# Hedgehog linear attention with a gated GLU on one core: the GLU's products in three passes over both chunks of tokens, with partial sums in DRAM

## The chip, the core and the metric

The kernel runs on one core of one Trainium2 chip. The core has five engines with a queue of instructions each: PE (TensorE, matmuls into the banks of PSUM), DVE (VectorE), ACT (ScalarE), POOL (GpSimd) and SP (SyncE, which issues the DMA transfers here). Each engine takes its own instructions strictly in order and waits on semaphores for those of the others. The metric is the device time of one execution in microseconds (us), as the median of several runs.

## What is computed

x has 2048 rows (tokens) of 1024 numbers. The layer norm of x feeds two branches that are multiplied at the end.

```python
xn  = layernorm(x)
# branch A: linear attention, 32 heads of 32
q, k, v = split(xn @ wqkv)
pq, pk  = per head: q @ w_phi, k @ w_phi
phi     = [softmax(p), softmax(-p)]          # 64 features for each head
kv, z   = phi_k.T @ v, sum(phi_k)            # over all 2048 tokens
s       = ((phi_q @ kv) / (phi_q @ z + 1e-6)) @ wo
# branch B: gated GLU, 1024 -> 3584 -> 1024
g   = silu((sigmoid(xn @ w_gate) * (xn @ w_up)) @ w_down)
out = x + s * g
```

All of it is in single precision. The sums over all tokens (kv, z) stand between the features of k and the rest of branch A.

## The kernel before

**Products.** Every factor of a large product is kept as two parts, a rounded high part and the rest (`split`, L128 to L131: an ACT cast makes the high part, L130, and a DVE subtraction the low one, L131). `mm3` (L133 to L137) multiplies with three matmuls: high by high, high by low, low by high. Each large product is cut in two along all three dimensions and done with seven block products in place of eight, named B11, T2, T3, B21, T1, T4, B22 (Strassen-Winograd). For that there are sums of blocks of the weights (made by POOL, `w_sums`, and stored in DRAM where they are used again), sums of blocks of the normalised x, and sums of results (DVE, while it empties the banks).

**Stages.** The 2048 tokens are two chunks of 1024. The order of the work is: projection of chunk 0 (V, K, Q), GLU of chunk 0, projection of chunk 1, GLU of chunk 1, the down product, then the attention's output and the store. The projection of chunk 0 with all that leads to it (loading, norm, transposes, folding w_phi into the weights of q and k) follows an order written out by hand, a list of short names, `FIRST` (L791 on); everything else is issued by loops and keeps the order of the program on each engine.

**The GLU of a chunk.** It runs over 14 column blocks j and two halves s. For each of these 28 pairs come the seven block products, each 12 matmuls of 512 columns into one bank from a ring of four. The factor from x lies in SBUF, split, for the whole chunk (28 slots of 512 KB, tiles x0 to x6). The weights go through eight slots (`w`, split, NW = 8): `prep` (L360) fills the next slot as soon as one is free. In chunk 0 it splits raw or summed weights and stores the four split sums to DRAM (`ws_d`); in chunk 1 it loads those four and splits the other three. Two partial sums u1 and u2 are kept in SBUF and added to by DVE from product to product (L1066 on); the gates, multiplications and sums of h blocks for the down product are ACT, DVE and POOL, and h goes to DRAM (`h_d`).

**Work in the background.** Beside the products run two lists of tasks, issued by `background` (L1008) behind a given DVE instruction. `bg` holds the features of q for chunk 0 and the transposing of x for chunk 1 (`q_features`, `x_task`, in the GLU of chunk 0), and then 32 `k_task`s (L462) with the sums behind them: for a tile of 128 tokens and half the heads it loads k and v, makes the two softmaxes (`features`, L440 to L457: maximum and minimum, two subtractions, exponential on ACT, a sum, a reciprocal), multiplies, splits p and v and adds to z. Its eight matmuls of 256 columns (`kv_products`, L481) are issued when the next task is issued. In the GLU of chunk 1 that is once in six products:

```python
            if m >= 1 and (m - 1) % 6 == 0:
                background(v.ins)
```

`bg2` holds sums of weights for wo and w_down (`o_sums`, `wd_sums`: four loads, four POOL operations, stores), one for each 14 products.

## Time and profile before

| | |
|---|---|
| time, median of 3 runs | 2377.14 us (2375.92 to 2377.75) |
| span of the profiled execution | 2376.2 us |
| mean granted TensorE clock | 1.00 |
| projection of chunk 0, from its first product's loads | about 14 to 286 us |
| GLU of chunk 0 | about 286 to 818 us |
| projection of chunk 1 | about 818 to 1053 us |
| GLU of chunk 1 | about 1053 to 1609 us |
| down product | about 1609 to 2128 us |
| attention and output | about 2128 us to the end |
| moved by DMA | 600 MB |

Engine rows of the page give busy time, share of the span and count of instructions. Rows of groups read: line, engine, operation, output<-input names, tile, count, busy us, mean ns of one, and what ended the idle time before them. Rows of waits read: waiting engine and line <- engine and line that released it, then the sum in us, the count and the longest. Rows of windows give the stretch, its length, the busy time (and count) of PE, weight load, DVE, ACT and POOL, the granted clock, the busy share of the DMA engines and GB/s. A bare timeline row gives start and duration in us. DMA rows give the count, the size of one and the median us from issue to landing.

### The profile page before, as it was taken

To read this page: it belongs to the slowest core of one execution; us is meant where nothing else is said; L and a number is where in the kernel's file an instruction comes from. 1 tells how busy PE (TensorE), PEld (TensorE's weight loads), DVE (VectorE), ACT (ScalarE), POOL (GpSimd) and SP (SyncE) were. 2 spreads that over 40 slices of the span, in tenths; PEclk is the share of its full clock that TensorE was granted. 3 is DMA by queue.
4 is the path that set the end of the run, shared out by engine and by line. 5 is a ranking of instruction groups with operands and counts; after the bars stand their busy time and mean duration, and the time that the engine had idled before them with its cause. 6 is when DMAs were issued, how large, how long until landed. Compare 5 with 4: busy or idle time off the path is not lost.

```text
span 2376.2 us, 31871 instructions
## 1 busy us (share of the span) xinstructions
PE 2361.1 (99%) x10972; PEld 1966.2 (83%) x10972; DVE 1778.2 (75%) x2340; ACT 1022.0 (43%) x1516; POOL 959.8 (40%) x613
## 2 busy tenths in 40 slices
PE   9999999999999999999999999999999999999999
PEld 8888888888888888888878888888888888888887
DVE  8626777877777575668884888865889998878776
ACT  7333344444434342324443444444444334455553
POOL 0223456666666433123443222232333334424566
PEclk9999999999999999999999999999999999999999
DMA  6689987778776787677777666668666666876665
GB/s 237 234 310 321 339 318 263 289 265 291 259 283 246 248 309 261 234 262 242 275 266 250 231 219 216 222 207 312 209 220 230 239 218 209 288 252 244 204 209 177
DMA packets 233587, 600.49 MB, mean 253 GB/s; under 512 B 30672, under 2 KB 30928, under 8 KB 228816
## 3 DMA queue, kind: packets, MB, share of 16 engines
q1 hardware_dynamic: 233424, 598.45, 72.3%
q8 instruction: 86, 1.41, 0.2%
q14 instruction: 77, 0.63, 0.1%
HBM read 363.20 MB, written 235.14 MB: 252 GB/s over the span
## 4 chain that ended last, share of the span: by engine, by line
PE 92%; DVE 4%; DMA 2%; issue 1%; ACT 1%; POOL 0%; SPq 0%; DVEq 0%; ACTq 0%
PE bank L135 29%; PE bank L137 29%; PE bank L136 29%; PE bank L696 1%; PE bank L672 1%; PE bank L486 1%; PE bank L285 1%; DMA fc<-wqkT 1%; DVE p L131 1%; DVE w L131 0%; DVE fc L450 0%; DVE fc L449 0%; DMA x<-x 0%; DMA fa<-wf_d 0%; DVE stk L453 0%
## 5 line engine op out<-in xcount | busy, mean ns | idle before, releaser
L136 PE MATMUL bank<-x,w 128*128 128x512 f32 x2352 | 915.7, 389 | 0.0
L135 PE MATMUL bank<-x,w 128*128 128x512 f32 x2352 | 909.8, 390 | 1.6 <-DVE fc L1073 1.1
L137 PE MATMUL bank<-x,w 128*128 128x512 f32 x2352 | 906.3, 390 | 0.0
L130 ACT CAST w<-fa 128x512 fp32r<-128x512 f32 (+1 forms) x430 | 294.8, 688 | 574.0 <-PE bank L136 365.9
L135 PEld LDWEIGHTS bank<-x,w 128*128 128x128 f32 x2352 | 441.6, 188 | 94.1 <-DVE fc L1073 2.3
L137 PEld LDWEIGHTS bank<-x,w 128*128 128x128 f32 x2352 | 441.5, 188 | 91.5 <-DVE w L131 0.4
L136 PEld LDWEIGHTS bank<-x,w 128*128 128x128 f32 x2352 | 441.6, 188 | 90.3
L131 DVE TENSOR_TENSOR w<-fa,w 128x512 fp32r<-128x512 f32 (+1 forms) x430 | 415.8, 972 | 104.1 <-ACT w L130 90.8
L135 PE MATMUL bank<-w,x 128*128 128x512 f32 x708 | 277.8, 393 | 0.2 <-ACT w L877 0.2
L136 PE MATMUL bank<-w,x 128*128 128x512 f32 x708 | 276.2, 390 | 0.9 <-DVE w L878 0.9
L137 PE MATMUL bank<-w,x 128*128 128x512 f32 x708 | 275.8, 390 | 0.0
L1089 POOL TENSOR_TENSOR fb<-fb,fc 128x512 f32<-128x512 f32 x57 | 89.0, 1561 | 291.6 <-DVE fc L1088 264.8
L137 PEld LDWEIGHTS bank<-w,x 128*128 128x128 f32 x708 | 132.9, 188 | 27.8 <-DVE x L868 0.3
L136 PEld LDWEIGHTS bank<-w,x 128*128 128x128 f32 x708 | 133.1, 188 | 27.4 <-DVE w L878 1.3
L135 PEld LDWEIGHTS bank<-w,x 128*128 128x128 f32 x708 | 133.1, 188 | 27.2 <-ACT w L877 0.6
L628 POOL TENSOR_TENSOR fc<-fc 128x1024 f32<-128x1024 f32 x32 | 81.4, 2542 | 173.7 <-ACT fc L451 125.4
L1088 DVE TENSOR_TENSOR fc<-fc,bank 128x512 f32<-128x512 f32 x84 | 57.5, 684 | 102.5 <-PE bank L137 97.4
L131 DVE TENSOR_TENSOR x<-fa,x 128x512 fp32r<-128x512 f32 x112 | 113.5, 1013 | 23.8 <-ACT x L130 23.6
L130 ACT CAST w<-fb 128x512 fp32r<-128x512 f32 x112 | 69.7, 622 | 141.7 <-PE bank L136 115.3
L131 DVE TENSOR_TENSOR p<-fc,p 128x1024 fp32r<-128x1024 f32 (+2 forms) x97 | 103.9, 1081 | 10.6 <-ACT p L130 8.3
L130 ACT CAST p<-fc 128x1024 fp32r<-128x1024 f32 (+2 forms) x97 | 70.7, 738 | 90.3 <-DVE fc L467 50.7
L640 POOL TENSOR_TENSOR fc<-fc,sa 128x1024 f32<-128x1024 f32 x32 | 70.4, 2199 | 90.6 <-DVE sa L637 90.6
(258 smaller groups left out, 3231.2 us busy)
## 6 DMA issues: line engine op xcount, KB each, us to landing
ws_d<-w SPq DMA_DIRECT2D x112, 512.0 KB, 4.2
w<-ws_d SPq DMA_DIRECT2D x112, 512.0 KB, 4.8
fa<-w_gu SPq DMA_DIRECT2D x84, 512.0 KB, 4.4
fa<-h_d SPq DMA_DIRECT2D x84, 512.0 KB, 4.0
fa<-wf_d SPq DMA_DIRECT2D x32, 1024.0 KB, 6.9
h_d<-fc SPq DMA_DIRECT2D x120, 256.0 KB, 3.2
fc<-e_d SPq DMA_DIRECT2D x48, 512.0 KB, 4.8
fc<-qkv_d SPq DMA_DIRECT2D x80, 256.0 KB, 4.3
```

The costliest lines, as they stand in the source:

```text
L130: nc.scalar.copy(o[0], src)
L131: return nc.vector.tensor_sub(o[1], src, o[0].bitcast(F32))
L135: nc.tensor.matmul(o, a[0], b[0], start=first, stop=False, **kw)
L136: nc.tensor.matmul(o, a[0], b[1], start=False, stop=False, **kw)
L137: nc.tensor.matmul(o, a[1], b[0], start=False, stop=last, **kw)
L285: nc.tensor.matmul(ps[:, gs], r[:, gs], bd[:, 4 * f + g], start=True, stop=True)
L486: nc.tensor.matmul(kvb[g // 2][:, g % 2 * 256:g % 2 * 256 + 256], v[:, g].rearrange("p a f -> p (a f)"), ph[:, g].rearrange("p a f -> p (a ...
L628: nc.gpsimd.tensor_mul(ez, e, zb)
L640: nc.gpsimd.tensor_mul(e3, e3, r2[:, :, None].to_broadcast([P, 32, DH]))
L672: nc.tensor.transpose(ps[:, j * P:(j + 1) * P], e[:, k * P:(k + 1) * P], ident)
L1088: v = nc.vector.tensor_add(b, u2 if q == 3 else u1, bank)
L1089: nc.gpsimd.tensor_mul(g, g, b)
```

## The change

The GLU is now made for both chunks of tokens together, product by product, in three passes over the 14 column blocks f:

- Pass 0 (after the projection of chunk 0): B11, B21 for each f, 28 units.
- Pass 1 (after the projection of chunk 1): T2, T3, T4, 42 units.
- Pass 2: T1, B22, 28 units.

A unit is one block product for both halves s and both chunks th of tokens: 48 matmuls into four fixed banks, with two weight slots, each used for both chunks. So each split weight serves both chunks: 196 splits where 280 stood, and no split weights in DRAM. `ws_d` gives way to `wg_d` for raw sums of weights, made by 28 new tasks in `bg2` (`glu_sums`: four loads, four POOL operations, four stores), which run from the projection of chunk 0 on to pass 1.

The factors from x are needed for both chunks at once, in three sets. Their raw blocks and sums go to DRAM in new stores (`xr_d`): 16 new entries X in the list `FIRST` and `outer_sums` in the `x_task`s. They come back through `load_outer` and `load_operand`: a load into a temporary slot (43 and 44, or 53 and 54) and a split.

The partial sums go to DRAM between the passes (`m_d`): after B11, T2 and T3 four ACT copies empty the banks and four stores keep them (`keep_banks`), `fetch` loads them a unit ahead, and T2 begins with four ACT copies of B11's sums into the banks. T3 and T4 go on in the same banks, B22 in T1's. `h_direct` (sigmoid on ACT, multiplication on DVE, straight from the banks) and `h_added` (four DVE additions of the kept sums, sigmoid, multiplication on POOL) make h.

The background moves too: `x_task`s go to pass 0, five k_tasks stay in the projection of chunk 1, the other 27 with the six tasks of sums go to the first 33 units of pass 1, one after each unit, and the 16 `q_features` to pass 2. `kv_products` still comes where the next task is issued, now one unit of 48 matmuls later. `bg2` has a task in two of three units of pass 1.

In all, the program has the same 10,846 PE instructions, 202 fewer of DVE (2,140), 112 more of ACT (1,630), four more of POOL (622), 416 more DMA issues on SP (2,015 instructions), and 658 MB of DMA in place of 598. In its code, line 134 is the DVE subtraction of `split`, 142 to 144 are `mm3`, and 482 is `kv_products`.

```diff
+    xr_d = dram.tile([7, P, CTT, HB], F32, name="xr_d")
+    wg_d = dram.tile([4, NJ, P, 2 * HB], F32, name="wg_d")
+    m_d = dram.tile([3, NJ, 4, P, HB], F32, name="m_d")
...
+    xtmp = Ring((43, 44))
+
+    def load_operand(first, raw, tmp=xtmp):
+        block(f"x{first // 4}", first, 4, F32R)
+        o = run(first, 4)
         for h in range(2):
-            r = (53, 54)[h]
-            nc.sync.dma_start(slots[r], xo_d[i, :, 2 * h:2 * h + 2])
+            r = tmp.next()
+            nc.sync.dma_start(slots[r], raw[:, 2 * h:2 * h + 2])
...
+    def load_outer(i, th):
+        load_operand(XG[i][th], xr_d[i, :, 4 * th:4 * th + 4])
...
+    PASSES = ((B11, B21), (T2, T3, T4), (T1, B22))
+    ops = [("proj", 0, which, i) for which in PROJ for i in order]
+    ops += [("glu", 0, f, i) for f in range(NJ) for i in PASSES[0]]
+    ops += [("proj", 1, which, i) for which in PROJ for i in order]
+    ops += [("glu", p, f, i) for p in (1, 2) for f in range(NJ) for i in PASSES[p]]
...
+    def glu_sums(f, s, bs):
+        cols = slice(s * HB, (s + 1) * HB)
+        for k, b in enumerate(bs):
+            nc.sync.dma_start(b, w_gu[f + NJ * (k // 2), k % 2, :, cols])
+        w_sums(lambda i, b: nc.sync.dma_start(wg_d[summed.index(i), f, :, cols], b) if i in summed else None, *bs)
...
-        kept = ws_d[u % (2 * NJ), summed.index(i)] if i in summed else None
-        if c and i in summed:
-            last_load[:] = [nc.sync.dma_start(slots[w].bitcast(F32), kept).ins]
-        else:
-            split(pair(w), wraw[u][i])
-            if i in summed:
-                nc.sync.dma_start(kept, slots[w].bitcast(F32))
+        glu_load(n)
+        glu_load(n + 1)
+        split(pair(w), slots[wraw[n]][:, len(ready[n])])
...
+    def keep_banks(m, f):
+        for b in range(4):
+            o = copies.next()
+            nc.scalar.copy(o, banks[b])
+            nc.sync.dma_start(m_d[m, f, b], o)
...
+            if c == 0 and i == T2:
+                load_outer(B11, 1)
+            if c:
+                m = order.index(i)
+                if m < 6:
+                    load_outer((T2, T2, T3, T3, T4, T4)[m], m % 2)
...
+        if i == T2:
+            for b in range(4):
+                nc.scalar.copy(banks[b], fetched[f][2][b])
+        if (phase, i) in ((1, T3), (2, T1)):
+            fetch(f + 1)
+        for s in range(2):
+            w = [h.rearrange("p (k m) -> p k m", m=P) for h in pair(ws[s])]
+            for th in range(2):
+                xo = run(XG[i][th], 4)
+                for k in range(4):
+                    mm3(banks[2 * s + th], (w[0][:, k], w[1][:, k]), (xo[:, k, 0], xo[:, k, 1]),
+                        i in (B11, T1) and k == 0, k == 3, skip_group_check=True)
...
+        elif phase == 1:
+            if len(bg) > 2 * CTT:
+                background()
+            if m >= 1 and m * 28 // 42 > (m - 1) * 28 // 42:
+                background2()
...
-            if m >= 1 and (m - 1) % 6 == 0:
-                background(v.ins)
+            if m >= 4:
+                background()
```

## The prediction

> **What bounds the kernel now.** I read the page first (busy shares, then the chain that ended last), then the waits of PE, then its raw timeline, because PE at 99% leaves only two ways to change the time: how long one matmul takes, and how long PE waits.

> ```profile
> span 2376.2 us, 31871 instructions
> PE 2361.1 (99%) x10972; PEld 1966.2 (83%) x10972; DVE 1778.2 (75%) x2340; ACT 1022.0 (43%) x1516; POOL 959.8 (40%) x613
> PE 92%; DVE 4%; DMA 2%; issue 1%; ACT 1%; POOL 0%; SPq 0%; DVEq 0%; ACTq 0%
> ```

> The chain is 92% PE. The waits of PE have columns of releaser: total us, count, longest. Among the eight listed, these four carry the terms below:

> ```profile
> PE bank L486 <- DVE p L131: 2.1, 2, 1.2
> PE bank L285 <- DMA fc<-wqkT: 2.1, 3, 1.6
> PE bank L135 <- DVE fc L1073: 1.1, 2, 0.9
> PE bank L135 <- DVE fb L1081: 0.4, 1, 0.4
> ```

> The timeline (start, duration) gives the pace: two GLU matmuls 88 steps apart, and a run of eight kv products.

> ```profile
> 499.98 0.39 PE L135 MATMUL bank<-x,w 128*128 128x512 f32 x1
> ...
> 519.93 0.39 PE L136 MATMUL bank<-x,w 128*128 128x512 f32 x1
> ...
> 1114.01 1.21 PE L486 MATMUL bank<-p,p 128*128 128x256 f32 x8 [0.93 <-DVE p L131]
> ```

> (519.93 − 499.98)/88 = 0.2267 us per 512-column matmul, though each record says 0.39: neighbours overlap by 0.16. A kv product has half the columns: 0.12 us as estimate (1.21 for eight with the last one's tail), so eight take 0.96.

> ```profile
> 1100.00:1250.00 150.00, 146.57 (x673) 121.25 (x671) 127.27 (x146) 68.40 (x86) 63.34 (x41) 1.00 0.77 263
> 190.00:290.00 100.00, 100.00 (x443) 82.80 (x442) 68.89 (x76) 39.14 (x57) 35.34 (x22) 1.00 0.93 335
> ```

> These windows list length, then busy us of PE, PEld, DVE, ACT, POOL, then clock, DMA share and GB/s. Where the k features run (1100 to 1250), DVE is the second engine, 127.27 of 150 us; the clock is 1.00.

> **The change, part by part.** *Matmuls.* PE has 10,846 instructions in both programs, with the same shapes: 0 us. Three of the waits above lie in the GLU of chunk 1: 2.1 + 1.1 + 0.4 = 3.6 us in five stalls; each also breaks an overlap of 0.16, so 4.4 us is all that the new order of the GLU can give back. I take all of it as gone: −4.4.

> *Splits and sums saved.* 196 weight splits stay of 280, and 140 DVE adds become copies or go. No PE wait names a GLU split (L131, W) now, so shorter work there is worth 0. What is bought with it is DVE room, spent below.

> *Where DVE's work goes.* This is the step that decides. Before, one k_task is issued per 6 products of 12 matmuls = 72; after, in pass 1, one per unit of 48, with its eight kv products at PE's next unit end. A unit lasts 48 × 0.2267 + 0.96 = 11.83 us on PE. kv_products (L482 after) wait for DVE's split of p and v; behind that wait stand all matmuls of the next unit, since PE is in order. So DVE's work per unit is compared with 11.83. Quiet durations, as steps from start to start on DVE's timeline:

> ```profile
> 1444.40 0.68 DVE L446 TENSOR_REDUCE stk<-fc 128x16 f32<-128x512 f32 x1
> 1444.99 0.68 DVE L447 TENSOR_REDUCE stk<-fc 128x16 f32<-128x512 f32 x1
> ...
> 1452.27 0.35 DVE L454 RECIPROCAL stk<-stk 128x32 f32<-128x32 f32 x1
> 1452.65 1.23 DVE L467 TENSOR_TENSOR fc<-fc,stk 128x1024 f32<-128x1024 f32 x1
> 1453.79 0.68 DVE L1073 TENSOR_TENSOR fc<-fc,bank 128x512 f32<-128x512 f32 x1
> ```

> A 512-wide instruction is 0.60 (1444.40 to 1444.99), a 1024-wide one 1.14 (1452.65 to 1453.79), the reciprocal 0.38. A k_task has five of the first (L446, 447, 449, 450, split of v), four of the second (L453, L467, L476, split of p), one reciprocal: 3.00 + 4.56 + 0.38 = 7.94. Add the unit's two W splits (1.20) and, in each third unit, two multiplications (0.40 on average): 9.54 us. On these alone DVE keeps pace. Two things come on top:

> ```profile
> L131 DVE TENSOR_TENSOR w<-fa,w 128x512 fp32r<-128x512 f32 x21 | 17.5, 832 | 0.0
> L131 DVE TENSOR_TENSOR p<-fc,p 128x1024 fp32r<-128x1024 f32 x8 | 14.1, 1763 | 0.0
> L476 DVE TENSOR_TENSOR fc<-fc 128x1024 f32<-128x1024 f32 x9 | 14.0, 1560 | 0.2
> L467 DVE TENSOR_TENSOR fc<-fc,stk 128x1024 f32<-128x1024 f32 x9 | 11.6, 1293 | 0.2
> L453 DVE TENSOR_REDUCE stk<-fc 128x32 f32<-128x1024 f32 x9 | 11.0, 1217 | 13.5 <-ACT fc L451 13.5
> L450 DVE TENSOR_TENSOR fc<-stk,fc 128x512 f32<-128x512 f32 x9 | 10.5, 1167 | 0.0
> L449 DVE TENSOR_TENSOR fc<-fc,stk 128x512 f32<-128x512 f32 x9 | 10.0, 1107 | 0.0
> L131 DVE TENSOR_TENSOR p<-fc,p 128x512 fp32r<-128x512 f32 x9 | 9.5, 1053 | 0.0
> L1088 DVE TENSOR_TENSOR fc<-fc,bank 128x512 f32<-128x512 f32 x9 | 6.1, 683 | 8.2 <-PE bank L137 8.2
> ```

> These are DVE's groups from 1100 to 1250 (count | busy us, mean ns | idle before).

> First, the reduce waits for the exponential: 13.5/9 = 1.5 us each time. In the new DVE order nothing stands between the subtractions (L450) and that reduce, so I keep 1.5. Bounds: 0 if something fills it, and 2.3 if the whole of ACT's table load and exponential is open:

> ```profile
> L451 ACT ACT_TABLE_LOAD x14 | 18.0, 1283 | 17.3 <-DVE fc L450 17.2
> L451 ACT ACTIVATE fc<-fc 128x1024 f32<-128x1024 f32 x16 | 17.0, 1063 | 13.1 <-DVE fc L450 12.9
> L1069 ACT COPY fc<-bank 128x512 f32<-128x512 f32 x16 | 9.3, 581 | 4.0 <-PE bank L137 4.0
> ```

> Second, the subtractions and splits run slower than quiet (0.68 for 512, 1.22 for 1024) while POOL works. Excess in this window: 21 × (832 − 680) + 8 × (1763 − 1220) + 9 × (1560 − 1220 + 1293 − 1220 + 1167 − 680 + 1107 − 680 + 1053 − 680) ns = 22.9 us, beside 63.34 us of POOL: 0.36 us of DVE per us of POOL. POOL's rows there:

> ```profile
> L575 POOL TENSOR_TENSOR fb<-fb,fb 128x512 f32<-128x512 f32 x4 | 7.4, 1838 | 0.2
> L576 POOL TENSOR_TENSOR fb<-fb 128x512 f32<-128x512 f32 x4 | 6.9, 1726 | 0.2
> L574 POOL TENSOR_TENSOR fb<-fb,fb 128x512 f32<-128x512 f32 x4 | 6.0, 1512 | 0.0
> L573 POOL TENSOR_TENSOR fb<-fb 128x512 f32<-128x512 f32 x4 | 5.9, 1476 | 4.5 <-DMA fb<-w_down 4.5
> ```

> Four sums take 1.84 + 1.73 + 1.51 + 1.48 = 6.6 us. Pass 1 has such a set (weight sums) in two of three units, 4.4, and four sums for h, about 6.6 again, in one of six, 1.1: 5.5 us of POOL per unit, so 5.5 × 0.36 = 2.0 us on DVE.

> DVE per unit: 9.54 + 1.5 + 2.0 = 13.04, against 11.83: 1.2 us short. 27 k_tasks run in pass 1 (eleven, three units of other work, sixteen); a task has about one unit of slack at the start of each run, which leaves some 24 that wait: 24 × 1.2 = +29 us at L482. Bounds: with 0 instead of 1.5, DVE needs 11.5 and nothing waits (0); with 2.3, 13.84 − 11.83 = 2.0, × 24 = +48.

> *ACT.* 112 instructions more, mostly copies of banks at 0.58 (L1069's row). Bank 0 is finished 36 matmuls = 8.2 us before the next unit wants it, so a copy has that as cover: 0. If ACT stands blocked at the exponential behind a late DVE, the copies are late with it, but that is the same lateness and not a second one.

> *SP and DMA.* 416 more issues on one queue, 658 MB instead of 598.

> ```profile
> qkv_d<-fc SPq DMA_DIRECT2D x18, 256.0 KB, 5.6
> ...
> fc<-qkv_d SPq DMA_DIRECT2D x23, 256.0 KB, 3.7
> ```

> Over pass 1's k_tasks I count 130 MB in 384 us, 339 GB/s. The window 190 to 290 carried 335 GB/s at 0.93 with PE busy all of it; there a 256 KB transfer landed in 5.6 us, 3.7 where it was calm (1300 to 1500). I take 0: W is split up to eight halves, four units, ahead (47 us), which also covers a store that waits for POOL ahead of a load in SP's queue. Without that cover, each load would cost its landing. The 16 stores of x in the opening stand among the weights of the first products, where PE waited 2.1 us in all (L285): 0 taken, up to 3.

> *The other stretches.* Pass 2 has per unit two splits, four adds and, in 16 of 28, a q_features (four 512-wide, one 1024-wide, one reciprocal: 3.9): 1.2 + 2.4 + 2.2 = 5.8 of DVE, and 6.6 of POOL (four instructions), so with 0.36 × 6.6 = 2.4 and the exponential's wait (0.9) 9.1 of 10.88: fits. Pass 0 and the second projection have less of both: 0. In Q's seven products (76 us) slots 43 and 44 serve four glu_sums of about 3.7 + 6.6 + 3.7 = 14 us (landing, sums, landing) and six load_outer of about 6 (landing and split, an estimate from the same rows), 92 us: the last operand, T4's, comes 16 us late, but is wanted two units (23 us) into pass 1: 0.

> Sum: 2376.2 − 4.4 + 29 = 2401 of span; the median shown, 2377.14, is 0.9 above the span: **2402**.

> **Rivals.** *DVE keeps pace* (the other side). If the exponential's wait is filled by a split of the coming unit, DVE needs 11.5 < 11.83. It decides at 11.83 per unit, only 1.2 from my sum. For it: the busy DVE rows of W need no exponential; against it: the order on DVE. 2376.2 − 4.4 + 0.9 = 2373, at the very edge of what a measurement tells from no change (0.2%, 4.8 us).

> *Entry of pass 1 late.* Slots 43/44 are a chain; if the two units of cover are gone, 16 us with DVE in pace: 2389. For it: 92 against 76; against: the early operands come first.

> *POOL blocks DVE outright.* The slowest of L449's 32 shows what one meeting can cost:

> ```profile
> L449 DVE TENSOR_TENSOR fc<-fc,stk x32: 676/686/1781, 880.0 to 1567.5; 128x512 f32<-128x512 f32 x32
> ```

> 1781 − 676 = 1.1 us. If each POOL instruction costs DVE that, 3.33 per unit give 3.7 instead of 2.0: 14.7 per unit, 2.9 × 24 = 70 us, 2442. Against it: the mean, 0.36 per POOL us, is a third of full blocking, and the median 686 is quiet.
> [...]

> **How the numbers follow.** My case 0.68, own range 2386 (half the deficit) to 2432 (the 48, and 10 for what DMA and the opening may add); DVE keeps pace 0.22, of it 0.10 faster by over 0.2% and 0.12 within; late entry 0.05; blocking 0.05. Slower: 0.68 + 0.10 = 0.78. The range 2373 to 2434 leaves out blocking, the faster part of the second case and a tail of mine, near 0.2.

> **What would show it.** In pass 1: PE's waits at L482 on DVE's split (L134 after), tens of us, a little over 1 per unit in the two runs of tasks and none in the three units between; DVE near 100% of that stretch; L453 still waiting 1.5 for ACT; no PE wait on W or on x; GLU waits of before gone; passes 0 and 2 at 0.2267 per matmul. Wrong if L482 waits little (something fills the exponential), if PE waits for DMA or for banks (ACT's copies), or if the opening grows by more than 3.

## The result, and the profile after

The changed kernel takes 2446.26 us (2444.71 to 2447.72) against 2376.69 us: a ratio of 1.0295, 95% interval 1.0281 to 1.031. It is slower, as forecast, but by 69.6 us where 25 were forecast, and outside the range.

The page of the changed kernel, the same rows as before (one by engine, and the chain, which this time was followed back only through a fifth of the span and so says little):

```profile
span 2445.3 us, 32192 instructions
PE 2386.3 (98%) x10972; PEld 1975.4 (81%) x10972; DVE 1672.1 (68%) x2138; ACT 1080.2 (44%) x1628; POOL 961.1 (39%) x617
PE 18%; DVE 2%; DMA 1%; issue 1%; ACT 0%; POOL 0%; ACTq 0%; DVEq 0%; SPq 0%
```

DVE has become less busy, as the saved splits and additions promise, and the kernel is slower: shares over the whole span hide the stage that decides. TensorE's waits (releaser, sum, count, longest) show it:

```profile
PE bank L482 <- DVE p L134: 31.9, 15, 4.4
PE bank L142 <- DVE x L1072: 8.1, 11, 1.0
PE bank L142 <- DVE fc L412: 4.1, 1, 4.1
PE bank L142 <- DVE fb L1072: 2.2, 3, 1.0
PE bank L142 <- DVE fc L1072: 2.2, 3, 1.0
PE bank L943 <- POOL ident masks.py:199: 1.5, 1, 1.5
PE bank L142 <- ACT bank L1129: 1.1, 2, 0.6
```

L482 are the kv products in pass 1, L1072 the additions of `h_added` in pass 2, L412 the sums of the second projection, in its last but one product before pass 1. The first is the wait that the prediction named; the other two it had put at nothing.

Some of these waits cost more than their length. The timeline of TensorE around one of them:

```profile
945.95 0.39 PE L144 MATMUL bank<-x,w 128*128 128x512 f32 x1
948.47 1.86 PE L482 MATMUL bank<-p,p 128*128 128x256 f32 x8 [2.14 <-DVE p L134]
950.13 0.63 PE L142 MATMUL bank<-x,w 128*128 128x512 f32 x1
950.56 0.63 PE L143 MATMUL bank<-x,w 128*128 128x512 f32 x1
950.98 0.63 PE L144 MATMUL bank<-x,w 128*128 128x512 f32 x1
951.41 0.63 PE L142 MATMUL bank<-x,w 128*128 128x512 f32 x1
951.84 0.56 PE L143 MATMUL bank<-x,w 128*128 128x512 f32 x1
952.23 0.40 PE L144 MATMUL bank<-x,w 128*128 128x512 f32 x1
952.47 0.40 PE L142 MATMUL bank<-x,w 128*128 128x512 f32 x1
```

After 2.14 us of waiting the steps are 0.43 us, twice the usual 0.2267, for 3.8 us; then the pace is back. Over the whole trace 53 matmuls of 512 columns and 51 of 256 run at that half pace: 53 x 0.20 + 51 x 0.108 = 16.1 us. About 14 us of this lie in pass 1, and 2 us behind the wait at L412.

Where the 69.1 us of span lie can be read from the steps between the starts of successive matmuls. Pass 1 has 34.6 (the waits at L482 with the overlaps that they break) + 14 at half pace = 49. Pass 2 has 15.4 (its 17 listed waits and one too short for the list, each with 0.16 of overlap) + 2.5 for a slow start behind each (a first step of 0.30 to 0.34 us in place of 0.2267, then a few up to 0.24) = 18. The end of the second projection has 4.2 + 2.4 at half pace = 6.6. Less the 4.4 of old GLU waits, all gone: 49 + 18 + 6.6 − 4.4 = 69. Small items on both sides (1.4 for the copies that put B11's sums back into the banks, some 3 fewer in the opening) cancel within what the lost records allow to say.

The stretch of pass 1's tasks, first the window (columns as before), then DVE's groups in it:

```profile
880.00:1230.00 350.00, 322.52 (x1450) 265.67 (x1449) 297.78 (x321) 203.36 (x296) 160.77 (x97) 0.97 0.87 300
```

```profile
L134 DVE TENSOR_TENSOR w<-fa,w 128x512 fp32r<-128x512 f32 x54 | 54.0, 999 | 7.2 <-ACT w L133 7.2
L134 DVE TENSOR_TENSOR p<-fc,p 128x1024 fp32r<-128x1024 f32 x24 | 40.5, 1686 | 0.0
L463 DVE TENSOR_TENSOR fc<-fc,stk 128x1024 f32<-128x1024 f32 x24 | 36.4, 1519 | 0.2
L472 DVE TENSOR_TENSOR fc<-fc 128x1024 f32<-128x1024 f32 x23 | 34.6, 1503 | 0.2
L449 DVE TENSOR_REDUCE stk<-fc 128x32 f32<-128x1024 f32 x24 | 29.3, 1220 | 38.3 <-ACT fc L447 38.3
L445 DVE TENSOR_TENSOR fc<-fc,stk 128x512 f32<-128x512 f32 x24 | 24.9, 1036 | 0.0
L134 DVE TENSOR_TENSOR p<-fc,p 128x512 fp32r<-128x512 f32 x26 | 24.0, 923 | 1.6 <-ACT p L133 1.6
L446 DVE TENSOR_TENSOR fc<-stk,fc 128x512 f32<-128x512 f32 x24 | 21.8, 910 | 0.0
```

The reduce (L449) still waits 38.3/24 = 1.6 us for the exponential, and is itself at its quiet 1220. The rest is over its quiet length (680 and 1220): 54 x 319 + 24 x 466 + 24 x 299 + 23 x 283 + 24 x 356 + 26 x 243 + 24 x 230 ns = 62.4 us beside 160.77 us of POOL, 0.39 per us. The DMA share is 0.87, below the 0.93 that the old opening carried.

### The profile page after: what moved, and what is told of

Same layout as the page of the kernel before. It is cut to its first block, busy times and chain, and to the rows that moved or that the text cites. A ratio compares the mean times of both kernels' runs of the same rounds, so it can differ in the third digit from the quotient of the medians.

```text
span 2445.3 us, 32192 instructions
## 1 busy us (share of the span) xinstructions
PE 2386.3 (98%) x10972; PEld 1975.4 (81%) x10972; DVE 1672.1 (68%) x2138; ACT 1080.2 (44%) x1628; POOL 961.1 (39%) x617
## 5 line engine op out<-in xcount | busy, mean ns | idle before, releaser
L142 PE MATMUL bank<-x,w 128*128 128x512 f32 x2352 | 922.4, 393 | 14.6 <-DVE x L1072 8.1
L134 DVE TENSOR_TENSOR w<-fa,w 128x512 fp32r<-128x512 f32 (+1 forms) x458 | 447.9, 983 | 280.4 <-ACT w L133 271.8
L142 PEld LDWEIGHTS bank<-x,w 128*128 128x128 f32 x2352 | 444.4, 189 | 115.5 <-issue 9.8
L133 ACT CAST w<-fa 128x512 fp32r<-128x512 f32 (+1 forms) x458 | 310.2, 681 | 503.1 <-PE bank L143 321.8
L142 PE MATMUL bank<-w,x 128*128 128x512 f32 x708 | 278.9, 394 | 4.1 <-DVE fc L412 4.1
L142 PEld LDWEIGHTS bank<-w,x 128*128 128x128 f32 x708 | 133.6, 189 | 31.4 <-DVE fc L412 5.0
L1037 ACT COPY fc<-bank 128x512 f32<-128x512 f32 x168 | 96.2, 583 | 87.9 <-PE bank L144 56.0
L134 DVE TENSOR_TENSOR x<-fa,x 128x512 fp32r<-128x512 f32 x112 | 114.7, 1024 | 27.7 <-ACT x L133 27.7
L260 POOL TENSOR_TENSOR fb<-fb 128x512 f32<-128x512 f32 x22 | 31.8, 1448 | 252.3 <-DMA fb<-w_gu 238.6
L134 DVE TENSOR_TENSOR p<-fc,p 128x1024 fp32r<-128x1024 f32 (+2 forms) x97 | 103.2, 1073 | 11.9 <-ACT p L133 8.4
L447 ACT ACTIVATE fc<-fc 128x1024 f32<-128x1024 f32 x64 | 67.9, 1061 | 94.8 <-DVE fc L446 90.1
L133 ACT CAST x<-fa 128x512 fp32r<-128x512 f32 x112 | 69.3, 618 | 77.4 <-DMA fa<-wd_d 34.7
## 6 DMA issues: line engine op xcount, KB each, us to landing
m_d<-fc SPq DMA_DIRECT2D x168, 256.0 KB, 4.8
x<-m_d SPq DMA_DIRECT2D x124, 256.0 KB, 4.7
h_d<-fc SPq DMA_DIRECT2D x114, 256.0 KB, 4.8
fc<-qkv_d SPq DMA_DIRECT2D x96, 256.0 KB, 4.7
```

The costliest lines, as they stand in the source:

```text
L133: nc.scalar.copy(o[0], src)
L134: i = nc.vector.tensor_sub(o[1], src, o[0].bitcast(F32))
L142: nc.tensor.matmul(o, a[0], b[0], start=first, stop=False, **kw)
L260: nc.gpsimd.tensor_add(a22, a21, a22)
L447: nc.scalar.activation(e, e, AF.Exp)
L1037: nc.scalar.copy(o, banks[b])
```

## The experiments

The theory was: in pass 1 VectorE needs longer for a unit than TensorE, because its own work, the exponential's wait and POOL's slowing add up. From the trace, 22 units of that stretch last 13.64 us on average: 9.44 quiet work of DVE, 1.65 of waiting for ScalarE, 2.53 of slowing, with 6.30 us of POOL (81 instructions in the 22 units, 66 of them sums of weights). The exponential's wait is the only idle time of note that VectorE has in them; over the whole of 894 to 1250 us it waited for TensorE 1.9 us in all. All runs below are variants of the changed kernel. A time without an interval is that of one run; the four runs of the changed kernel lie within 3.0 us.

**POOL's sums left out of pass 1**

```diff
-        nc.gpsimd.tensor_add(a22, a21, a22)
...
+        if phase[0] != 1:
+            nc.gpsimd.tensor_add(a22, a21, a22)
...
```

(The same around the four operations of `wd_sums`.)

> The changed kernel without the four POOL operations of each task of weight sums in pass 1; its loads and stores stay (the summed weights are left out, so the output is not the reference's). My theory: POOL's 4.4 us per unit cost VectorE 0.36 us each, 1.6 us per unit; 13.6 falls to 12.0 against 11.83, the waits at L482 fall from 34.6 to under 10 us and the half clock mostly goes: about 2408, range 2398 to 2420. Rival, VectorE is slow for another reason (transfers): no change, 2446. Rival, POOL blocks VectorE fully, 1.1 us per instruction: 2.67 instructions per unit are 2.9 us, VectorE falls to 10.6 and no wait is left: 2396.

Measured: 2403.92 us. DVE's groups of this run from 880 to 1180, and a window of it:

```profile
L135 DVE TENSOR_TENSOR w<-fa,w 128x512 fp32r<-128x512 f32 x53 | 39.4, 743 | 8.3 <-ACT w L134 8.2
L135 DVE TENSOR_TENSOR p<-fc,p 128x1024 fp32r<-128x1024 f32 x23 | 28.1, 1221 | 1.2 <-ACT p L134 1.2
L451 DVE TENSOR_REDUCE stk<-fc 128x32 f32<-128x1024 f32 x23 | 28.1, 1220 | 41.2 <-ACT fc L449 41.2
L465 DVE TENSOR_TENSOR fc<-fc,stk 128x1024 f32<-128x1024 f32 x23 | 28.0, 1217 | 0.2
...
L448 DVE TENSOR_TENSOR fc<-stk,fc 128x512 f32<-128x512 f32 x23 | 16.8, 731 | 0.0
L447 DVE TENSOR_TENSOR fc<-fc,stk 128x512 f32<-128x512 f32 x23 | 16.8, 729 | 0.0
```

```profile
880.00:1030.00 150.00, 150.00 (x704) 125.76 (x703) 114.96 (x157) 98.80 (x150) 16.07 (x10) 1.00 0.99 353
```

The split of p falls from 1686 to 1221 ns, the subtractions from 1036 and 910 to 730, and TensorE is busy all of the window. This is one edit on POOL alone, with all its transfers kept: 42 us of the loss hang on POOL's sums beside DVE. (Their stores no longer wait for POOL either, but in the changed kernel VectorE's tasks waited only 0.3 us for their loads, L442 from 880 to 1250.) The same row excludes transfers as the bound: at a DMA share of 0.99 and 353 GB/s TensorE did not wait. Over 21 units of this run the slowing is 0.44 us, 2.09 less than with the sums, for the 66/22 = 3.0 sums of weights in a unit: about 0.7 us each, between the 0.36 x 1.65 = 0.6 of my sum and the 1.1 of the blocking rival.

**The tasks of k spread over pass 1**

```diff
-            if len(bg) > 2 * CTT:
+            if m >= 1 and m * 34 // 42 > (m - 1) * 34 // 42:
                 background()
```

> The changed kernel with the 33 tasks of k issued in 33 of all 42 units of pass 1 (a free unit after each three or four) instead of in its first 33. My theory: VectorE cannot do a task and the unit's own work in the unit's 11.83 us (13.6 us per unit in the trace), so TensorE waits at L482; with the free units in between the mean falls to about 10.7 us per unit. Then most of the 34.6 us lost at L482 goes, and the 14 us at half clock with it: 2446 to about 2410, range 2400 to 2422. Rival 1, each task by itself is late whatever its neighbours are: 27 tasks lose as before, 2440 to 2447. Rival 2, pass 1 is bound by transfers: no change, 2446.

Measured: 2431.92 us, 14 less, between theory and rival 1. The wait:

```profile
PE bank L482 <- DVE p L134: 21.5, 14, 4.3
```

Where the free units put 16 us or more between two runs of kv products, waits not counted, none waits from 840 us on; the waits stand where it is 13 us or less. Whether these tasks are late by themselves, for POOL's sums in their units, or by the tasks just before them, this run does not tell. I had reasoned with a mean over units; what counts is each task against the one unit until its products.

**The split of v put into the exponential's wait**

```diff
+        nc.scalar.copy(v[:, :, 0], vr)
+        r = features(f"k{t}{hb}", kraw, e_k,
+                     lambda: nc.vector.tensor_sub(v[:, :, 1], vr, v[:, :, 0].bitcast(F32)))
...
         nc.scalar.activation(e, e, AF.Exp)
+        if between is not None:
+            between()
```

> The changed kernel with the split of v put into the wait for the exponential: its cast ahead of the exponential on ScalarE, its subtraction between the two subtractions and the sum on VectorE. My theory: the wait of 1.6 us per task is part of VectorE's pace, and 0.6 of it is filled; 24 tasks x 0.6 = 14 us less at L482: about 2432, range 2425 to 2440. Rival, the cast ahead delays the exponential by as much as is filled: 2446. Rival, VectorE's pace is not the bound: 2446.

Measured: 2446.36 us, nothing. The reduce waits as long as before with the subtraction of v now ahead of it:

```profile
L451 DVE TENSOR_REDUCE stk<-fc 128x32 f32<-128x1024 f32 x24 | 29.3, 1220 | 38.9 <-ACT fc L447 38.9
```

So the first rival fits: the cast of v, now ahead of the exponential on ScalarE, puts that off by what is filled. The second rival gives the same time, and only the run without POOL's sums speaks against it. That the wait is part of DVE's pace is not tested by this edit, since it did not shorten it.

**q_features moved to pass 0**

```diff
-    qf_raw, qf_e = Ring(halves(52)), Ring((53, 54))
+    qf_raw, qf_e = Ring(halves(36)), Ring((37, 38))
...
+            if m >= 12:
+                background(bgq)
...
-            if m >= 4:
-                background()
```

> The changed kernel with the 16 q_features moved from pass 2 to the last 16 units of pass 0. My theory: the 18 us lost in pass 2 (waits at L142 on the additions L1072) come from the additions that stand behind the exponential's wait on VectorE, and pass 0 has room: about 2428, range 2424 to 2432. Rival, the loss moves to pass 0, where B21 waits for VectorE too: 2440 to 2450. Rival, the additions are late by themselves: 2446.

Measured: 2432.79 us, 13.5 less. No wait is left in pass 2, whose waits cost 18; some 2.5 us came back in pass 0, where the norm of x is late (3.0 us of waits), and about 1 us in pass 1. The list has 4.7 more at L482 there (36.6), but less of pass 1 runs at half pace; the run of added matmuls below comes back to this. What the additions stood behind is seen on DVE's timeline in pass 2 of the changed kernel:

```profile
1511.26 1.78 DVE L446 TENSOR_TENSOR fc<-stq,fc 128x512 f32<-128x512 f32 x1
1512.96 0.67 DVE L1072 TENSOR_TENSOR fb<-fb,bank 128x512 f32<-128x512 f32 x1
1515.49 1.22 DVE L449 TENSOR_REDUCE stq<-fc 128x32 f32<-128x1024 f32 x1 [1.86 <-ACT fc L447]
1516.63 0.68 DVE L1072 TENSOR_TENSOR fb<-fb,bank 128x512 f32<-128x512 f32 x1
```

One addition is done, then DVE stands 1.86 us for the exponential and 1.2 in the reduce, and only then comes the addition that empties the next bank. TensorE, just starting the next unit, needs that bank 12 x 0.2267 = 2.7 us after the first.

**No weight sums in Q's products**

```diff
-            if (i in (T2, T3, T1, B22)) if c else n in (12, 14, 16, 18):
+            if (i in (T2, T3, T1, B22) and what != Q) if c else n in (12, 14, 16, 18):
...
-            if m >= 1 and m * 28 // 42 > (m - 1) * 28 // 42:
+            if m >= 1 and m * 30 // 42 > (m - 1) * 30 // 42:
```

> The changed kernel without tasks of weight sums in Q's products of the second projection (their four follow in pass 1, where they run in 30 of 42 units instead of 28). My theory: the wait of 4.1 us at the end of Q's products, and the 2.4 us that TensorE loses at half clock and in the ramp behind it, come from slots 43 and 44, in which weight sums and the raw factors of x wait for each other, and VectorE stands behind a load; both go, 6.5 us, and one or two more tasks beside the k tasks give 3 back: 2443, range 2439 to 2445. Rival, the factors of x are late by themselves: 2446 to 2449.

Measured: 2442.15 us, and the wait at L412 is gone. DVE in the changed kernel, without that edit, and then the first of the two casts on ScalarE:

```profile
791.35 0.69 DVE L412 TENSOR_TENSOR fc<-fc,bank 128x512 f32<-128x512 f32 x1
801.68 1.23 DVE L134 TENSOR_TENSOR x<-fb,x 128x1024 fp32r<-128x1024 f32 x1 [9.65 <-ACT x L133]
805.37 1.23 DVE L134 TENSOR_TENSOR x<-fb,x 128x1024 fp32r<-128x1024 f32 x1 [2.46 <-ACT x L133]
806.51 0.68 DVE L412 TENSOR_TENSOR fc<-fc,bank 128x512 f32<-128x512 f32 x1
```

```profile
800.60 1.05 ACT L133 CAST x<-fb 128x1024 fp32r<-128x1024 f32 x1 [10.92 <-DMA fb<-xr_d]
```

The load of a factor of x waits for the weight sums in its slot (POOL ends the last one at 795.3 us, the load is issued at 795.77), ScalarE's cast for the load, DVE's subtraction for the cast, and behind it stand the sums that empty the projection's banks. The factor itself was in time.

**TensorE kept at work while it waits**

```diff
             t, ph, v = kv_due.popleft()
+            for a in range(8 if t and phase[0] == 1 else 0):
+                nc.tensor.matmul(kvb[a % 4][:32], zero, run(4 * 6, 1)[:, 0, 0], start=False, stop=False, skip_group_check=True)
```

> The changed kernel with eight more matmuls of 512 columns (zeros times a factor of x, added to the kv banks, so nothing changes in them) ahead of each run of kv products in pass 1: TensorE works 1.8 us where it would wait. Theory A, VectorE sets the pace of the k units and the half clock behind a wait only uses up waiting time: the half clock goes nearly, L482 waits about 1 us less each, and the time stays within 2441 to 2454 (units that do not wait now pay 1.8 us, some 10 of them, partly taken off later waits). Theory B, the 14 us at half clock stand on top of the waits: 2428 to 2438. Theory C, TensorE sets the pace and the added matmuls all count: 26 x 1.8 = 47, 2480 to 2493.

Measured: 2458.8 us, 5 above theory A's band and far from B's and C's. Of the 47 us of added matmuls 35 went into time that was there already.

```profile
PE bank L487 <- DVE p L137: 7.0, 3, 3.5
```

The half pace falls from 16.1 to 5.6 us and the loss at the kv products (L487 here) from 34.6 to 7.5. From 1080 on no unit waits; each lasts 13.5 to 14.0 us, which is TensorE's own 11.83 + 1.81 = 13.64. That this equals the 13.64 of the changed kernel is chance, and it keeps the run from telling theory A from theory B: with the added 47 us, a kernel with no loss at all in pass 1 would take 2446 − 49 + 47 = 2444, so the band of B could not be reached. The 12 us that came on top I put down to units that had been shorter than 13.6, as some in the changed kernel are (11.2 to 12.6); that is read from the lengths, not tested.

What tells them apart is the run with q_features in pass 0. Pass 1 has the same work there. From the first run of kv products after 890 us to the last one it takes as long in both; first the changed kernel, then that run:

```profile
894.45:1247.50 353.05, 320.88 (x1445) 263.71 (x1443) 299.86 (x321) 203.51 (x296) 163.01 (x99) 0.96 0.86 297
898.95:1252.65 353.70, 317.57 (x1445) 261.50 (x1443) 302.25 (x322) 204.09 (x296) 164.20 (x99) 0.98 0.86 297
```

The clock stands at half for about 26 us of the first and 17 us of the second (the 0.96 and 0.98), and TensorE waits at L482 for 31.5 and 36.1 us. Less half pace was made up by more waiting, at the same pace. So in pass 1 the half pace took up time in which TensorE would have waited, as theory A has it.

**All moves together**

```diff
-    EARLY = (4, 7, 11, 14, 18)
+    EARLY = (1, 3, 5, 7, 9, 11, 13, 16)
...
-            if len(bg) > 2 * CTT:
+            if m >= 1 and m * 31 // 42 > (m - 1) * 31 // 42:
                 background()
-            if m >= 1 and m * 28 // 42 > (m - 1) * 28 // 42:
+            if m % 2 == 1:
                 background2()
```

With this, q_features in pass 0, `wd_sums` in pass 0 and pass 2, and no sums in Q's products.

> The changed kernel with the work around it moved by what was found: q_features in pass 0, eight k tasks in the second projection instead of five, the other 30 tasks in 30 of the 42 units of pass 1, the sums of w_down in pass 0 and pass 2 instead of pass 1, no weight sums in Q's products. My theory: with POOL's sums and the tasks spread, VectorE's mean in pass 1 is about 10 us per unit against 11.83, so L482 keeps under 8 us, the 18 us of pass 2 go, and the entry's 6.5 go: 2446 - 27 - 12 - 18 - 6 = 2383, range 2374 to 2395. Rival, single k tasks stay late even when spread (21.5 us were left at L482 when they were only spread): 2395 to 2412. If it lies under 2377, it beats the kernel before.

Measured: 2415.86 us, 1.0168 (1.0138 to 1.0197), above the range. What was aimed at came: L482 has 1.3 us left and pass 2 loses one wait of 1.8. A new wait undid most of it:

```profile
PE bank L142 <- ACT x L133: 26.6, 1, 26.6
```

At the end of pass 0 the loads for the second projection stood in SyncE's queue behind stores of `wd_sums` and `q_features` that waited for POOL, for DVE and most of all for ScalarE's exponential (11.3 us in five waits from 560 to 622 us).

**The same, with three places mended** (the lines are against the run before)

```diff
-            if m >= 12:
-                background(bgq)
-            if m >= 13 and m % 2:
-                with tc.issue_after(last_load[0]):
-                    background(bg3)
+            if 4 <= m < 20:
+                background(bgq)
...
-            if m % 3 == 1:
+            if m >= 5 and m % 2 or m in (24, 26):
                 with tc.issue_after(last_load[0]):
                     background(bg3)
...
-        nc.gpsimd.memset(m, 0.0)
+        nc.vector.memset(m, 0.0)
```

> The run before (e8_best) with three places mended that its trace shows: the sums of w_down all in pass 2 and q_features in units 4 to 19 of pass 0, so that the loads for the second projection no longer stand behind their stores in SyncE's queue (a wait of 26.6 us at 619 us); the clearing of the kv blocks on VectorE instead of POOL (2.9 us); nothing of w_down in the first units of pass 2 (1.8 us). My theory, all three and the half clock behind them go: 2416 - 27 - 3 - 3 - 2 = 2381, range 2374 to 2388, so the changed GLU comes out within half a per cent of the kernel before, not clearly ahead of it. Rival, the loads at the end of pass 0 are late by themselves: 2400 to 2416. Rival, the sums of w_down slow pass 2: 2388 to 2400.

Measured: 2387.75 us (2383.12 to 2390.36), 1.0040 of the kernel before (1.0026 to 1.0054), at the upper edge of the range. The waits that are left are all small; the three largest:

```profile
PE bank L503 <- ACT fc L501: 2.3, 1, 2.3
PE bank L142 <- ACT x L133: 2.1, 1, 2.1
PE bank L482 <- DVE p L134: 1.9, 2, 1.1
```

So 58.5 of the 69.6 us were the placing of the work around the GLU's products, and not the three passes, the partial sums in DRAM or their transfers. The other 11 us were not taken apart. No variant beat the kernel before.

## Why the prediction was wrong

*The sign, the place and the mechanism held.* TensorE waits at L482 for the split of p, in 15 of the runs of kv products; W and transfers gave no wait in pass 1, and the banks 1.1 us. The 4.4 us of old GLU waits went, the opening did not grow, and the transfers were hidden: 300 GB/s in the stretch shown, where I had counted 339, and 353 still passed without a wait in the run without POOL's sums.

*The step that failed first: "DVE per unit 13.04", times 24.* It is 13.64 over the 22 units above. From 894.45 to 1006.17 and from 1043.97 to 1247.50 us lie 23 units in 315.25 us, 43 us more than 23 x 11.83 = 272, instead of 29; the rest of pass 1's 49 is mostly half pace behind the last wait of each run of tasks, and short waits ahead of them. So the count of 24 was near, and the shortfall per unit was mis-sized, 1.2 for some 1.9. The quiet work was right (9.44 for 9.54), the exponential 1.65 for 1.5; the error is POOL's term, 2.53 for 2.0. POOL worked 6.30 us per unit and not 5.5: 3.68 instructions for 3.33, of 1.71 us on average for 1.65. Each us of it cost 0.39 to 0.41, not 0.36. The slack at the start of a run of tasks was there, and more than the one unit that I had counted: in the second run the first three kv products do not wait and the fourth waits 3.12 us.

*The step "pass 2 fits: 0" failed*: 18 us. The sum of DVE's work per unit, 9.1 of 10.88, was not the question. The additions stand in order behind the exponential's wait, and a bank is wanted at a moment, not within a unit.

*The step "T4's factor comes 16 us late: 0" failed*, 6.6 us, though its premise was right: the chain through slots 43 and 44 was late. I asked who reads the factor and not who is queued behind the split that waits for it, the question which I had put to L482.

*ACT as the same lateness* held: the copies that put B11's sums into the banks lost 1.4 us in all.

*The rivals.* Late entry came, in another form and beside the forecast case. The blocking rival gave 2442, near the measured time, but as a mechanism it is not what the runs show: about 0.7 us per POOL instruction against its 1.1, and pass 1 gave 49 us against its 70; pass 2 and the entry make up the difference. Without POOL's sums the slowing all but disappears (the split of p from 1686 to 1221 ns, a subtraction from 1036 to 729), and the reduce is the same 1220 in both.

*What I had not priced at all* is the half pace behind waits. It was no cost of its own in pass 1 (the same length with 26 and with 17 us of it), but behind the single wait at L412 it cost 2 us.

## What to carry to other kernels

Before spreading background work by a mean over a stage, set each task against the time until its consumer, with the slowest company that it can meet on the other engines (here the split of p took 1686 ns beside POOL's sums and 1221 without them). For each wait that a moved instruction may have, list what is queued behind it on its own engine, on SyncE too: here a split waiting for a load, an exponential's wait and a store each held up work that was itself in time (TensorE waited 4.1, 12.5 and 26.6 us). Saved busy time on an engine that is not the bound need not bring anything: here VectorE's fell from 1778.2 to 1672.1 us over the whole span, and the time rose by 69.6.

## What the runs showed of the hardware

Behind some waits of TensorE its matmuls run at half pace for 2.7 to 5.7 us: after 2.14, 2.18, 2.72, 2.93, 3.12, 4.08, 4.35 and 4.42 us, but not after 2.08, nor after one of 3.15 us, so length alone does not decide it. The two rows of kv products show both cases: 1.86 us for eight after the wait of 2.14, and

```profile
1165.00 1.22 PE L482 MATMUL bank<-p,p 128*128 128x256 f32 x8 [3.15 <-DVE p L134]
```

What tells the two apart in this trace is where the wait lies. The granted clock in the trace of the changed kernel has eight stretches at 0.50 before its last microseconds. They begin at 805.40, 948.76, 965.83, 1006.79, 1081.88, 1136.49, 1204.76 and 1245.72 us, always a whole number of steps of 3.413 us apart, and last one or two such steps. Rows of windows on that grid, for the wait of 2.14 us and then for that of 3.15 us:

```profile
945.35:948.76 3.41, 1.27 (x7) 0.77 (x6) 3.41 (x3) 0.75 (x2) 1.98 (x1) 1.00 0.82 278
948.76:952.17 3.41, 3.41 (x13) 3.02 (x13) 3.41 (x5) 1.10 (x2) 1.66 (x1) 0.50 0.63 219
1160.38:1163.80 3.42, 1.48 (x7) 0.90 (x5) 3.39 (x3) 2.23 (x4) 1.24 (x1) 1.00 1.03 394
1163.80:1167.21 3.41, 2.21 (x13) 2.01 (x14) 3.41 (x5) 0.31 (x1) 0.88 (x2) 1.00 0.86 262
```

Transfers at a share of 0.99 and 353 GB/s left TensorE without a wait for 150 us (880 to 1030 in the run without POOL's sums), where the loads are issued units ahead.
